# An FFT layer with eight experts behind it: which sorted tile each step of the expert stage works on

## The chip, the cores and the metric

The kernel runs as one program on one core of a Trainium2 chip. The metric is the device time of one execution in microseconds (us), and a kernel's time is the median of its runs. Engines are named as in the profile: PE (TensorE matmul) with PEld (its weight load), DVE (VectorE), ACT (ScalarE), POOL (GpSimd) and SP (SyncE), which here only issues transfers; SPq and POOLq are the sequencers that feed them.

## The reference

Eight sequences of 2496 rows with 256 features go through a Fourier transform along the sequence, a complex 256x256 matrix with bias, a soft threshold and the transform back. Each of the 19968 rows that come out is then sent to one of eight experts, two matrices 256x1024 and 1024x256 with a relu between them, and weighted.

```
X = rfft(x, axis=1)
Yr, Yi = Xr @ w_r - Xi @ w_i + b_r,  Xr @ w_i + Xi @ w_r + b_i
Yr, Yi = soft(Yr, 0.01), soft(Yi, 0.01)
x = irfft(Yr + 1j * Yi).reshape(19968, 256)
e_idx = argmax(x @ w_gate, axis=1)
for e in range(8):
    m = e_idx == e
    out[m] = gate_w[m] * sigmoid(x[m] @ w_output_gate[:, e]) * (relu(x[m] @ w1[e]) @ w2[e])
```

Run on its own inputs, the reference sends 1122, 1344, 1215, 1226, 1333, 1194, 1064 and 1486 rows of the first four sequences to experts 0 to 7, and 2254, 2696, 2453, 2444, 2626, 2443, 2081 and 2971 rows of all eight.

## The kernel before, in words

Values are held as pairs of f16 numbers (a high and a low part), so a product is three matmuls. The Fourier part runs first, sequence by sequence, and writes its rows to `yd` in DRAM. Beside it the expert matrices are scaled, split and written to `wd` in DRAM, 2 MB an expert. The expert stage begins about a third into the program.

**Sorting.** Rows are sorted by expert into tiles of 128. Phase A covers the first four sequences: each expert's rows fill whole pairs of tiles (count // 256 of them), and the first 64 tiles so filled, 32 pairs, are worked on while the last sequences are still being finished. Phase B holds all that is left, each expert's share rounded up to whole tiles, in 99 tiles. So there are 163 tiles (`T_ALL`), worked on in 131 blocks (`BLOCKS`, L41): 32 of two tiles and 99 of one. Which tile number stands for which sorted position is decided by a row of numbers on the chip: tile t takes sorted position t of phase A, or t - 64 of phase B. `plan` (L1062) compares these positions with each expert's start (L1088 to L1092) and so gets `eb`, the expert of each tile; `routing` (L1200) compares the tile number in which a row belongs with the same numbers (`line`, L1224), and the index tables `gidx` and `sidx` for the gathers and scatters come out of that.

**Blocks.** A block gathers the rows of its tiles from `yd` (`gathers`, L1319, an indirect DMA from POOL at L1327), scales and splits them on ACT and DVE (`tokens`, L1333), and turns them with a DMA transpose from SP into `eT` (L1366). `up` (L1447) multiplies with the first matrix (PE, L1458), ACT and DVE make `hh` of it (L1468, L1469), `down` (L1414) multiplies with the second (PE, L1424), ACT scales the result (L1440), and POOL scatters it to the output rows (L1443). In phase B PE's order is two blocks' `up`, then the two `down` of the pair before.

**Weights.** An expert's 2 MB lie in one of three places in SBUF, `wbuf0` to `wbuf2` (`W`); `wplace` (L1291) names the place of block k: blocks 0 to 3 alternate between places 0 and 1, and from block 4 on blocks go round the three. Block k's place was last used by block k - 3 (`before`, L1294). `fetch` (L1298) issues two transfers of 1 MB for each block from SP (L1313), the first half (for `up`) after the earlier block's `up`, the second after its `down`. Each is conditional: a flag in `fl` says whether the block's expert differs from that of the place's earlier block (L1099 to L1104). With the flag at 0 the instruction is issued and moves nothing. SP takes its instructions in program order, and the transposes of L1366 stand between these transfers.

The order of all instructions is worked out ahead by a small simulator in the program (`Issue`), from fixed costs and due times; it doesn't depend on the data.

Of the kernel before, what the change touches and what calls it, by code (L numbers as in the profile page):

```python
# [18 lines left out]
ALU = mybir.AluOpType  # L19
# [5 lines left out]
B, S, D, E, DF = 8, 2496, 256, 8, 1024  # L25
# [3 lines left out]
P3 = 3 * N1  # L29
# [7 lines left out]
T_A = -((-(NA * S - E * 255)) // 256) * 2  # L37
T_B = (N - E) // 128 + E - T_A
T_ALL = T_A + T_B
BLOCKS = [(t, 2) for t in range(0, T_A, 2)] + [(t, 1) for t in range(T_A, T_ALL)]  # L40


def _split(t):
# [4 lines left out]
def tables():  # L48

    n1 = np.arange(N1)  # L50
    k1 = np.arange(K1)
    n2 = np.arange(N2)
    k2 = np.arange(N2)
    a1 = 2 * np.pi * np.outer(n1, k1) / N1
    f1 = np.zeros((3, N1, K1, 3, 2))
    f4 = np.zeros((K1 // 2, 3, 2, 2, 3, N1))
    for s in range(3):
        f1[s, :, :, s, 0] = np.cos(a1)
        f1[s, :, :, s, 1] = -np.sin(a1)
        f4[:, s, :, 0, s, :] = np.cos(a1).T.reshape(K1 // 2, 2, N1)  # L60
        f4[:, s, :, 1, s, :] = -np.sin(a1).T.reshape(K1 // 2, 2, N1)
    f1 = f1.reshape(P3, 120).astype(np.float32)
    f4 = np.concatenate(_split(64 * f4.reshape(120, P3)), axis=1)
    c = np.zeros((128, K1, 128))
    g = np.zeros((128, K1, 128))
    for k in range(K1):
        th = 2 * np.pi * (np.outer(n2, k + 39 * k2) % S) / S
        co, si = np.cos(th), np.sin(th)
        cj = np.where((k2 >= 32) & (k > 0), -1.0, 1.0)
        use = np.where((k == 0) & (k2 > 32), 0.0, 1.0)  # L70
        c[:, k] = np.block([[co * use, -si * use * cj], [si * use, co * use * cj]])
        wr = np.ones(N2)
        wi = np.ones(N2)
        if k == 0:
            wr[33:] = 0.0
            wi[32:] = 0.0
            wi[0] = 0.0
            wr[0] = wr[32] = 0.5
        g[:, k] = np.block([[co.T * wr[:, None], si.T * wr[:, None]], [-si.T * (wi * cj)[:, None], co.T * (wi * cj)[:, None]]])

    mix = np.array([64 * c + 22 * s + q for q in range(NQ) for s in range(3 if q < 20 else 2) for c in range(2)])
    c, g = c[mix], g[:, :, mix]
    ch, cl = _split(64 * c)
    cmat = np.stack([ch, cl], axis=2).reshape(128, K1 * 2 * 128)
    gh, gl = _split(64 * g)
    gmat = np.stack([gh, gl], axis=2).reshape(128, K1 * 2 * 128)

    t = np.zeros((128, NCOL), np.int64)
    real = np.zeros((128, NQ))
    for s in range(3):  # L90
        nq = NQ - 2 * (s > 1)
        rows = slice(s * N1, (s + 1) * N1)
        real[rows, :nq] = 1
        for b in range(B):
            v = 64 * n1[:, None] + np.arange(NQ)[None, :] + 22 * s - S // 2
            t[rows, b * NQ:(b + 1) * NQ] = v + (v >= 0)
    t *= np.tile(real, B).astype(np.int64)
    m16 = np.zeros((128, M16), np.float16)
    m16[:P3, :P3] = np.triu(np.ones((P3, P3)), 1)
    m16[:P3, 128:256] = 1  # L100
    m16[:, 256:432] = t
    m16[:, 432:608] = (real[:, :, None] * (8 - np.arange(8))).reshape(128, 176)
    m16[:, 608:M16 - 384] = np.arange(128 * CB) // CB
    m16[:, M16 - 384:M16 - 256] = np.arange(128)
    m16[:, M16 - 256:M16 - 128] = np.eye(128)

    m16[0:64:32, M16 - 128:M16 - 64] = 2.0 ** 7
    m16[64:128:32, M16 - 64:] = 2.0 ** 7
    return dict(
        f1=np.ascontiguousarray(f1),  # L110
        f4=np.ascontiguousarray(f4),
        cmat=np.ascontiguousarray(cmat),
        gmat=np.ascontiguousarray(gmat),
        m16=m16,
    )
# [36 lines left out]
KW = 4  # L152
# [16 lines left out]
CB = 4  # L169
OL = 2, 3  # L170
KP = 2
NP = K1 // KP
M16 = 608 + 128 * CB + 128 + 256


class Slots:
# [109 lines left out]
def tile_fft_moe(ctx, tc, x, w_r, w_i, b_r, b_i, w_gate, w_og, w1, w2, f1, f4, cmat, gmat, m16, out, dbg=None):  # L286
# [46 lines left out]
    t16 = pc.tile([128, M16], F16, name="t16")  # L333
# [45 lines left out]
    ones = t16[:P3, 128:256]  # L379
    va = t16[:P3, 256:432]  # L380
    eye = t16[:, M16 - 256:M16 - 128]
    iota = t16[:, 608:M16 - 384].rearrange("p (j c) -> p j c", c=CB)
    line = t16[:P3, M16 - 384:M16 - 256].rearrange("p (c j) -> p c j", c=1)
    sel = t16[:, M16 - 128:M16]

    def absmax(m, src):
# [675 lines left out]
    def plan(ph):  # L1062

        if ph == 0:
            fl = shift(cnt[NA - 1], 0, 8, "fl")
            yield
            pf_ = yield from prefix(fl, "pfA")
            lim = small(E + 1, "lim", pool=pc)
            V.tensor_scalar(pf_, pf_, 2.0, None, ALU.mult)
            V.tensor_scalar(lim, pf_, float(T_A), None, ALU.min)  # L1070
            n1 = small(E, "n1", pool=pc)
            V.tensor_tensor(n1, lim[:, 1:], lim[:, :E], ALU.subtract)
            route["n1"] = n1
            off, bound, start = pf_[:, :E], lim[:, 1:], lim
        else:
            ce = shift(cnt[B - 1], 127, 7, "ce")
            V.tensor_tensor(ce, ce, route["n1"], ALU.subtract)
            yield
            start = yield from prefix(ce, "pfB")
            off_ = small(E, "offB", pool=pc)  # L1080
            V.tensor_tensor(off_, start[:, :E], route["n1"], ALU.subtract)
            off, bound = off_, start[:, :E]
        yield
        route[ph] = off, bound
        n = (T_A, T_B)[ph]
        t0 = T_A * ph
        ev = eb[:, t0:t0 + n]
        V.tensor_scalar(ev, iota[:, :n, 0], start[:, 1:2], None, ALU.is_ge)  # L1088
        for e in range(2, E):
            V.scalar_tensor_tensor(ev, iota[:, :n, 0], start[:, e:e + 1], ev, ALU.is_ge, ALU.add)  # L1090
            if e % 2:
                yield  # L1092
        if ph == 0:
            route["fl"] = pc.tile([1, T_ALL], I32, name="flg")
            route["ei"] = pc.tile([1, T_ALL], I32, name="ebi")
            V.memset(route["fl"][:, 0:2 * KW + 1], 1)
        V.tensor_copy(route["ei"][:, t0:t0 + n], ev[0:1])
        fl = lambda a, b, c, d, step: V.tensor_tensor(route["fl"][:, a:b], eb[0:1, a:b], eb[0:1, c:d:step], ALU.not_equal)
        if ph == 0:  # L1099
            fl(4, 2 * KW, 0, 2 * KW - 4, 1)  # L1100
            fl(2 * KW + 1, T_A, 2 * KW - 5, T_A - 6, 1)
        else:
            fl(T_A, T_A + 3, T_A - 6, T_A, 2)
            fl(T_A + 3, T_ALL, T_A, T_ALL - 3, 1)  # L1104
# [95 lines left out]
    def routing(ph, r, gap):  # L1200

        nb = (NA, B)[ph]
        n = (T_A, T_B)[ph]
        yield "ranked", nb - 1
        yield from parts(plan(ph), "D", r, 0.7)
        io.set("plan", ph)
        if ph:
            yield "opened"
            yield "tiles", 0
        for b in range(0, nb, 2):  # L1210
            yield from parts(blocks(ph, b, min(2, nb - b)), "D", r, 0.5)
        io.set("blocks", ph)
        pool = (psm, pools.get("h"))[ph]
        for b in range(nb):
            for q in range(0, NQ, CB):
                m = min(CB, NQ - q)
                yield slots[f"ol{ph}"]
                ol = ring(pool, [P3, 128, CB], F16, f"ol{ph}", OL[ph])
                ob = ring(pool, [P3, CB, n], F16, f"ob{ph}", OL[ph])
                cs = slice(b * NQ + q, b * NQ + q + m)  # L1220
                lc = rlo[:, cs].rearrange("p (o c) -> p o c", o=1).broadcast_to([P3, 128, m])
                bc = blk[:, cs].rearrange("p (c o) -> p c o", o=1).broadcast_to([P3, m, n])
                yield "D", r, 0.147 * m, lambda: V.tensor_tensor(ol[:, :, :m], iota[:P3, :, :m], lc, ALU.is_equal)
                yield "D", r, 0.115 * m, lambda: V.tensor_tensor(ob[:, :m], line[:, :, :n].broadcast_to([P3, m, n]), bc, ALU.is_equal)  # L1224
                io.go(columns(ph, b, q, m, r, ol, ob))
                r += gap * m
                yield max(gap * m - 1.2, 0.0)
        while st.get(("cols", ph), 0) < nb * NQ:
            yield 1.0
        yield slots["gL"]  # L1230
        yield from parts(indices(ph), "D", r, 0.6)
        give("gL")
        io.set("ix", ph)
        for i in range(-(-nb // (512 // n))):
            io.free(route["map", ph, i][0])
        if ph == 0:
            yield "weights"
        yield from parts(factors(ph), "D", r, 0.51)
        io.set("tiles", ph)
# [47 lines left out]

    def place(k, i, shape, dt):
        return pools["w" if i < EARLY[k] else "h"].tile(shape, dt, tag=f"{k}{i}", name=f"{k}{i}")

    def wplace(k):  # L1291
        return k % 2 if k < KW else (k - KW + 2) % 3

    def before(k):  # L1294

# [230 lines left out]
```

## Time and profile before

| | |
|---|---|
| median of three runs | 1447.63 us (1446.49 to 1449.62) |
| the profiled execution: its own time, its span | 1450.28 us, 1448.5 us |
| mean granted TensorE clock | 0.993 |
| busy: PE, PEld, DVE | 1402.4, 1273.4, 978.5 us |
| busy: ACT, POOL | 737.0, 636.1 us |
| `wbuf<-wd` instructions | 262, of 1024 KB each where they move something |
| start of the first and of the last matmul of the expert stage | 552.0 and 1444.0 us |

A row of the timeline gives the start in us, the length in us, the engine, the line, the operation with its output and inputs, the shape and the number of instructions merged; in square brackets stands how long the engine was idle before it and what ended that. A row of the waits gives the engine and line that waited, what released it, the us in total, the times and the longest wait. A row of the windows gives a stretch, its length, the busy time of PE, PEld, DVE, ACT and POOL, the granted clock, the share of the DMA engines' time in use and the GB/s that they moved.

### The profile page before, as it was taken

How to read it: one execution, taken by the hardware profiler on the slowest of the kernel's cores; microseconds unless marked ns; L12 is line 12 of the kernel's file. 1: busy time of each engine (PE TensorE's matmuls, PEld its weight loads, DVE VectorE, ACT ScalarE, POOL GpSimd, SP SyncE). 2: the span in 40 equal slices, each digit the busy share in tenths (PEclk: the TensorE clock that was granted, in tenths of full speed). 3: DMA queues.
4: the chain of work that ended last, by engine and by line, in shares of the span. 5: the costliest groups of instructions: out<-in, count | busy, mean ns of one | idle time of the engine just before them, and what ended most of it. 6: DMA issues, size and time to landing. Idle time of an engine off the chain costs nothing.

```text
span 1448.5 us, 42626 instructions
## 1 busy us (share of the span) xinstructions
PE 1402.4 (97%) x16436; PEld 1273.4 (88%) x16436; DVE 978.5 (68%) x2796; ACT 737.0 (51%) x1413; POOL 636.1 (44%) x729
## 2 busy tenths in 40 slices
PE   4999999999999999999999999999999999999998
PEld 4998887888888888888888888999999999989998
DVE  4888767788998896788888855545545455445452
ACT  4777675778687764433333333333333333333342
POOL 2274565355577563345554333333343333333321
PEclk8999999999999999999999999999999999999999
DMA  7779899998988789977795789674838568386520
GB/s 197 174 174 217 205 224 211 220 223 216 218 211 202 177 238 197 285 193 199 232 231 145 215 207 264 168 218 111 245 94 227 160 167 242 81 244 194 126 58 24
DMA packets 294005, 276.47 MB, mean 191 GB/s; under 512 B 241847, under 2 KB 250169, under 8 KB 282026
## 3 DMA queue, kind: packets, MB, share of 16 engines
q1 hardware_dynamic: 277239, 229.68, 62.5%
q0 software_dynamic: 15872, 42.83, 12.3%
q8 instruction: 129, 2.11, 0.6%
q10 hardware_dynamic: 690, 1.24, 0.3%
q14 instruction: 75, 0.61, 0.1%
HBM read 337.44 MB, written 58.91 MB: 274 GB/s over the span
## 4 chain that ended last, share of the span: by engine, by line
PE 45%; issue 29%; POOL 14%; DVE 6%; DMA 2%; ACT 2%; SPq 1%; POOLq 0%; ACTq 0%; DVEq 0%
PE ps L731 11%; PE ps L1458 9%; PE ps L1424 8%; POOL out L1443 7%; POOL yg L1327 7%; PE ps L623 5%; PE ps L761 3%; PE ps L827 3%; PE ps L701 3%; DMA x<-in_x 1%; PE ps L872 1%; PE ps L666 1%; PE ps L725 1%; PE ps L1253 1%; DVE z L747 1%
## 5 line engine op out<-in xcount | busy, mean ns | idle before, releaser
L1458 PE MATMUL ps<-eT,wbuf 128*128 128x128 f16 (+1 forms) x6288 | 460.9, 233 | 8.4 <-DMA wbuf<-wd 5.6
L1424 PE MATMUL ps<-wbuf,hh 128*128 128x256 f16 x3912 | 453.8, 273 | 0.6 <-DMA wbuf<-wd 0.6
L1458 PEld LDWEIGHTS <-wbuf 128*128 128x128 f16 x6288 | 419.2, 98 | 30.0 <-DMA wbuf<-wd 7.2
L1424 PEld LDWEIGHTS <-hh 128*128 128x128 f16 x3912 | 378.9, 98 | 45.7 <-issue 1.3
L1469 DVE SCALAR_TENSOR_TENSOR hh<-ps,hh 128x512 f16<-128x512 f32 x326 | 224.9, 690 | 275.8 <-ACT hh L1468 275.6
L1468 ACT ACTIVATE hh<-ps 128x512 f16<-128x512 f32 x326 | 194.6, 597 | 294.3 <-PE ps L1458 287.9
L1443 POOL DMA_INDIRECT out<-o,sidx x163 | 163.4, 1003 | 283.4 <-ACT o L1440 259.7
L1327 POOL DMA_INDIRECT yg<-yd,gidx x163 | 161.5, 991 | 252.4 <-DVE yhl L1353 218.2
L731 PE MATMUL ps<-whl,xt 128*128 128x256 f16 x1920 | 223.1, 273 | 0.7 <-ACT xt L716 0.7
L731 PEld LDWEIGHTS <-xt 128*128 128x128 f16 x1920 | 187.6, 98 | 32.2 <-ACT xt L716 1.1
L1440 ACT ACTIVATE o<-ps,facs 128x256 f32<-128x256 f32 x163 | 77.2, 473 | 229.1 <-PE ps L1424 138.4
L1353 DVE SCALAR_TENSOR_TENSOR yhl<-yg,ys,yhl 128x256 f16<-128x256 f32 x163 | 81.8, 508 | 66.2 <-ACT yhl L1352 66.1
L623 PEld LDWEIGHTS ps<-f1t,x 117*128 117x128 f32 (+1 forms) x704 | 86.4, 199 | 18.2 <-issue 15.9
L623 PE MATMUL ps<-f1t,x 117*128 117x120 f32 (+1 forms) x704 | 89.9, 284 | 0.2 <-ACT ste L778 0.2
L1352 ACT ACTIVATE yhl<-yg,ys 128x256 f16<-128x256 f32 x163 | 81.7, 501 | 13.9 <-DVE ys L396 6.2
L751 POOL TENSOR_TENSOR zhl<-z,zhl 128x512 f16<-128x512 f32 x54 | 62.7, 1162 | 52.4 <-ACT zhl L749 50.0
L1028 POOL TENSOR_TENSOR wsp<-wr,wsp 128x512 f16<-128x512 f32 x62 | 74.3, 1198 | 5.2
L761 PE MATMUL ps<-gt,zhl 128*128 128x128 f16 x960 | 65.7, 220 | 7.9 <-DVE zhl L751 3.4
L761 PEld LDWEIGHTS <-zhl 128*128 128x128 f16 x960 | 58.6, 98 | 15.0 <-DVE zhl L751 4.2
L827 PE MATMUL ps<-bdt,f4t 120*117 120x512 f16 x264 | 70.6, 383 | 0.1
L632 ACT ACTIVATE at<-ps,sx 128x480 f16<-128x480 f32 (+1 forms) x88 | 55.7, 650 | 29.1 <-PE ps L623 25.9
L633 DVE SCALAR_TENSOR_TENSOR at<-ps,sx,at 128x480 f16<-128x480 f32 (+1 forms) x88 | 59.3, 696 | 12.5 <-ACT at L632 12.3
(195 smaller groups left out, 1647.8 us busy)
## 6 DMA issues: line engine op xcount, KB each, us to landing
wbuf<-wd SPq DMA_DIRECT2D x262, 1024.0 KB
yd<-yt SPq DMA_DIRECT2D x120, 158.4 KB
x<-in_x SPq DMA_DIRECT2D x114, 156.0 KB
wr<-in_moe_w SPq DMA_DIRECT2D x32, 512.0 KB
wd<-wsp SPq DMA_DIRECT2D x64, 256.0 KB
yg<-yd,gidx POOLq DMA_INDIRECT x163
eT<-yhl SPq DMA_TRANSPOSE x163
out<-o,sidx POOLq DMA_INDIRECT x163
```

The costliest lines, as they stand in the source:

```text
L623: T.matmul(pv[:, dh, :, m * j:m * j + m], xs[:k, j0 + j, 128 * dh:128 * dh + 128], fw, start=True, stop=True)
L731: T.matmul(yp[:, 256 * j:256 * j + 256], xt_[:, v, 2 * dh + j, 64 - 64 * u:192 - 64 * u], whl[:, dh, vw, 256 * u:256 * u + 256], start=Fal ...
L761: T.matmul(bv[:, j], zhl[:, vz, c:c + 128], gt[:, 2 * p + j, v], start=(n == 0), stop=(n == 2))
L827: T.matmul(pt[:P3], w, src[:, :, :, vb_], start=(n == 0), stop=(n == 2))
L1327: yield "G", r + 5.6 * t - 30, 1.0, lambda: G.indirect_dma_start(out=yg, out_offset=None, in_=src, in_offset=bass.IndirectOffsetOnAxis(ap= ...
L1352: yield "A", r - 10, 0.5, lambda: A.activation(yhl[:, 0], yg[:, :256], AF.Copy, scale=s)
L1353: yield "D", r - 10, 0.48, lambda: V.scalar_tensor_tensor(yhl[:, 1], yg[:, :256], s, yhl[:, 0], ALU.mult, ALU.subtract)
L1424: T.matmul(st["pt", t][1][:, :256], hh[:, v, fc, 128 * n:128 * n + 128], w[:, fc // 2, vw, fc % 2], start=(fc == k == 0), stop=(fc == 7 an ...
L1443: yield "G", r - DN, 1.0, lambda: G.indirect_dma_start(out=outs[t % 8], out_offset=bass.IndirectOffsetOnAxis(ap=sidx[:, t:t + 1], axis=0), ...
L1458: T.matmul(pt[:, 128 * m * j:128 * m * (j + 1)], w[:, dh, g // 4, vw, 128 * (g % 4):128 * (g % 4) + 128], eT[:, :m, v, dh], start=(n == 0) ...
L1468: yield "A", r, 0.6, lambda: A.activation(hv[:, 0], pt, AF.Relu)
L1469: yield "D", r, 0.69, lambda: V.scalar_tensor_tensor(hv[:, 1], pt, 0.0, hv[:, 0], ALU.max, ALU.subtract)
```

## The change

The tiles of each phase are handed out otherwise. A new table, `streams()`, gives each tile its sorted position so that the blocks of one place, taken by themselves, run through one third of the sorted tiles: in phase A place 0 gets the first third in order, place 1 the second and place 2 the last; in phase B the same thirds backwards, so that a place enters phase B near the sorted position at which it left phase A. The table is stored in the constant input `m16` where the plain numbers 0 to 127 stood, and both comparisons (for `eb` and in `routing`) read it. `wplace` moves out of the kernel function, unchanged. Flags, fetches, `before` and everything else stay.

```diff
+KA = T_A // 2
...
-    m16[:, 608:M16 - 384] = np.arange(128 * CB) // CB
-    m16[:, M16 - 384:M16 - 256] = np.arange(128)
+    m16[:, 608:LINE] = np.arange(128 * CB) // CB
+    m16[:, LINE:LINE + T_ALL] = streams()
...
-M16 = 608 + 128 * CB + 128 + 256
+LINE = 608 + 128 * CB
+M16 = LINE + T_ALL + T_ALL % 2 + 256
+
+
+def wplace(k):
+    return k % 2 if k < KW else (k - KW + 2) % 3
+
+
+def streams():
+
+    order = np.zeros(T_ALL, np.int64)
+    g = 0
+    for p in range(3):
+        for k in range(KA):
+            if wplace(k) == p:
+                order[2 * k:2 * k + 2] = g, g + 1
+                g += 2
+    g = 0
+    for p in range(3):
+        for k in reversed(range(KA, len(BLOCKS))):
+            if wplace(k) == p:
+                order[BLOCKS[k][0]] = g
+                g += 1
+    return order
...
-    line = t16[:P3, M16 - 384:M16 - 256].rearrange("p (c j) -> p c j", c=1)
+    line = t16[:, LINE:LINE + T_A], t16[:, LINE + T_A:LINE + T_ALL]
...
-        V.tensor_scalar(ev, iota[:, :n, 0], start[:, 1:2], None, ALU.is_ge)
+        V.tensor_scalar(ev, line[ph], start[:, 1:2], None, ALU.is_ge)
...
-            V.scalar_tensor_tensor(ev, iota[:, :n, 0], start[:, e:e + 1], ev, ALU.is_ge, ALU.add)
+            V.scalar_tensor_tensor(ev, line[ph], start[:, e:e + 1], ev, ALU.is_ge, ALU.add)
...
-                yield "D", r, 0.115 * m, lambda: V.tensor_tensor(ob[:, :m], line[:, :, :n].broadcast_to([P3, m, n]), bc, ALU.is_equal)
+                yield "D", r, 0.115 * m, lambda: V.tensor_tensor(ob[:, :m], line[ph][:P3].rearrange("p (c j) -> p c j", c=1).broadcast_to([P3, m, n]), bc, ALU.is_equal)
```

On every engine the instructions stand in the same order as before. One row differs in anything but its line number: SP's load of the constant table, where `t` is the tile `t16` and `in_m` the input `m16`. Before, near the head of SP's program:

```order
6 L359 DMA ct<-in_cmat 128x2560
7 L329 DMA x_278<-in_x 39x1024 x3
8 L363 DMA t_82<-in_m 128x1248
9 L364 DMA wgr<-in_moe_w_gate 128x2x8
10 L365 DMA wgr<-in_moe_w_output_gate 128x2x8
```

and with the change:

```order
6 L383 DMA ct<-in_cmat 128x2560
7 L353 DMA x_278<-in_x 39x1024 x3
8 L387 DMA t_82<-in_m 128x1284
9 L388 DMA wgr<-in_moe_w_gate 128x2x8
10 L389 DMA wgr<-in_moe_w_output_gate 128x2x8
```

The table's load is 36 columns wider, and nothing moved. What changes are numbers: which of the conditional transfers move data, and which rows each gather and scatter takes.

More of the change, by code (lines that the diff above doesn't have):

```diff
@@ L381, in tile_fft_moe @@
     eye = t16[:, M16 - 256:M16 - 128]
-    iota = t16[:, 608:M16 - 384].rearrange("p (j c) -> p j c", c=CB)
-    line = t16[:P3, M16 - 384:M16 - 256].rearrange("p (c j) -> p c j", c=1)
+    iota = t16[:, 608:LINE].rearrange("p (j c) -> p j c", c=CB)
+    line = t16[:, LINE:LINE + T_A], t16[:, LINE + T_A:LINE + T_ALL]
     sel = t16[:, M16 - 128:M16]
@@ L1289, in place @@
         return pools["w" if i < EARLY[k] else "h"].tile(shape, dt, tag=f"{k}{i}", name=f"{k}{i}")
-    def wplace(k):
-        return k % 2 if k < KW else (k - KW + 2) % 3
     def before(k):
```

## The prediction

> **What bounds the kernel now.** First the page: which engine is full, and how much is transferred.
>
> ```profile
> PE 1402.4 (97%) x16436; PEld 1273.4 (88%) x16436; DVE 978.5 (68%) x2796; ACT 737.0 (51%) x1413; POOL 636.1 (44%) x729
> PEclk8999999999999999999999999999999999999999
> DMA packets 294005, 276.47 MB, mean 191 GB/s; under 512 B 241847, under 2 KB 250169, under 8 KB 282026
> q1 hardware_dynamic: 277239, 229.68, 62.5%
> HBM read 337.44 MB, written 58.91 MB: 274 GB/s over the span
> ```
>
> PE is busy 97% of the span at nearly full clock. The change removes transfers and no matmul, so it can gain only what PE loses while it waits for transfers, however many megabytes go. Hence the next view, PE's waits over the whole span, with the longest one for scale and the three that concern the expert stage:
>
> ```profile
> PE ps L422 <- DVE dg L418: 17.6, 4, 10.5
> ...
> PE ps L1458 <- DMA wbuf<-wd: 5.6, 5, 2.2
> ...
> PE ps L1458 <- DMA eT<-yhl: 2.7, 1, 2.7
> ...
> PE ps L1424 <- DMA wbuf<-wd: 0.6, 1, 0.6
> ```
>
> So the ceiling is small: 5.6 + 0.6 us for weights and, if transposes wait behind weights, 2.7 us more. PE's timeline shows where these are and what follows them. First phase A, where a block's `up` begins with the rows of L1458 x24:
>
> ```profile
> 839.98 2.78 PE L1458 MATMUL ps<-eT,wbuf 128*128 128x256 f16 x24
> ...
> 847.84 2.78 PE L1424 MATMUL ps<-wbuf,hh 128*128 128x256 f16 x24
> 853.34 4.16 PE L1458 MATMUL ps<-eT,wbuf 128*128 128x256 f16 x24 [2.72 <-DMA eT<-yhl]
> ...
> 865.49 2.78 PE L1458 MATMUL ps<-eT,wbuf 128*128 128x256 f16 x24
> ...
> 875.97 2.78 PE L1458 MATMUL ps<-eT,wbuf 128*128 128x256 f16 x24
> ```
>
> An undisturbed pair takes 875.97 - 865.49 = 10.48 us. The pair before the wait took 853.34 - 839.98 = 13.36 us, 2.88 too many; the one behind it 12.15 us, 1.67 too many, with no wait in it. Its first 24 matmuls took 4.16 us against 2.78. The windows show why:
>
> ```profile
> 840.00:850.00 10.00, 10.00 (x94) 8.96 (x92) 5.84 (x20) 4.10 (x9) 4.51 (x5) 1.00 1.01 259
> ...
> 855.00:857.00 2.00, 2.00 (x11) 1.45 (x10) 0.69 (x1) 0.58 (x1) 0.00 (x0) 0.50 0.98 398
> ...
> 1292.00:1296.00 4.00, 3.92 (x60) 3.80 (x61) 1.68 (x4) 1.59 (x3) 0.33 (x1) 1.00 0.93 330
> ```
>
> After the 2.72 us wait the granted clock (third number from the end) is 0.50; after the longest weight wait, 2.21 us at 1292, it stays 1.00. So the long wait costs 2.88 + 1.67 = 4.55 us. The Trainium skill, TensorE: Matmul & The Clock Gate, Part 1, puts the fall to half clock behind an idle window of about 3.4 us; by that the 1.67 us would not hang on this wait and would stay, and the gain below would be 1.67 us smaller. Here the clock did fall after 2.7 us, so the row decides and I count it.
>
> Phase B, every place where PE waited for weights, and undisturbed rows for the pace (two blocks' `up` begin at each x96 row):
>
> ```profile
> 925.48 2.85 PE L1458 MATMUL ps<-eT,wbuf 128*128 128x128 f16 x48 [0.70 <-DMA wbuf<-wd]
> 928.92 5.40 PE L1424 MATMUL ps<-wbuf,hh 128*128 128x256 f16 x48 [0.59 <-DMA wbuf<-wd]
> 934.16 5.52 PE L1458 MATMUL ps<-eT,wbuf 128*128 128x128 f16 x96
> ...
> 977.34 5.53 PE L1458 MATMUL ps<-eT,wbuf 128*128 128x128 f16 x96 [0.53 <-DMA wbuf<-wd]
> ...
> 1226.10 2.85 PE L1458 MATMUL ps<-eT,wbuf 128*128 128x128 f16 x48 [1.56 <-DMA wbuf<-wd]
> ...
> 1292.08 2.85 PE L1458 MATMUL ps<-eT,wbuf 128*128 128x128 f16 x48 [2.21 <-DMA wbuf<-wd]
> ...
> 1343.32 5.53 PE L1458 MATMUL ps<-eT,wbuf 128*128 128x128 f16 x96 [0.56 <-DMA wbuf<-wd]
> ...
> 1353.93 5.52 PE L1458 MATMUL ps<-eT,wbuf 128*128 128x128 f16 x96
> ...
> 1428.13 5.52 PE L1458 MATMUL ps<-eT,wbuf 128*128 128x128 f16 x96
> 1433.49 5.40 PE L1424 MATMUL ps<-wbuf,hh 128*128 128x256 f16 x48
> ```
>
> From 1353.93 to 1428.13 nothing waits: 7 pairs of blocks in 74.20 us, 10.60 a pair. From 934.16 to 1428.13 there are 46 pairs, 487.6 us at that pace, and it took 493.97: phase B loses 6.4 us, all around the changes of expert (the four waits sum to 4.9, the rest is restarts and waits under half a microsecond).
>
> **What the change does to the transfers.** From the reference's counts, phase A has 4, 5, 4, 4, 5, 4, 4 and 2 pairs for experts 0 to 7, phase B has 10, 12, 12, 12, 11, 12, 9 and 20 tiles and one empty tile. Before, a change of expert runs through all places: blocks 0, 1, 4 and then 19 more fetch in phase A, 3 for each of 8 experts in phase B: 22 + 24 = 46 blocks, 92 transfers of 1 MB. The page agrees: a transfer is 128 packets of 8 KB, 92 x 128 = 11,776, and it has 294005 - 282026 = 11,979 packets of 8 KB or more, some 200 of them instructions. After, places 0, 1 and 2 hold 11, 11 and 10 pairs, so experts 0-1-2, 2-3-4 and 5-6-7: 9 fetches. In phase B, backwards, 33 tiles each, place 0 runs 2-1-0 (2 is there already), place 1 5-4-3-2 (4 was there), place 2 7-6-5 (7 is there): 2 + 4 + 2 = 8. So 17 blocks fetch and 29 stop fetching, at 2.1 MB each 60.8 MB less. The new ones are blocks 0, 1, 4, 6, 11, 16, 18, 26 and 28, then 33, 60, 65, 93, 97, 101, 124 and 129: no two neighbours after the first two, and in phase B at least four blocks, 21 us, apart.
>
> **Is a lone fetch hidden?** A place is used by every third block, so between its last use and the next one PE has two whole blocks, 10.6 us in phase B and 21 us in phase A, and each half has this room for itself. The first fetch of a group before is such a lone one. For block 101, whose `up` began inside 1276.43's row:
>
> ```profile
> 1266.76 2.31 SPq L1313 DMA_DIRECT2D wbuf<-wd  x2
> ...
> 1269.50:1274.00 4.50, 4.50 (x60) 4.21 (x58) 3.70 (x13) 1.59 (x3) 0.99 (x1) 1.00 0.86 263
> ...
> 1276.43 5.52 PE L1458 MATMUL ps<-eT,wbuf 128*128 128x128 f16 x96
> ```
>
> The second of these instructions, near 1269.0, is its first half; at 263 GB/s 1.05 MB take 4.0 us, so it was there by 1274, five microseconds before need, and no first block of a group shows a wait of a microsecond. Only second and third blocks do, since 6.3 MB at about 295 GB/s take 21 us. After the change there are none of those.
>
> **The sum, against the profiled execution's 1450.28 us** (span 1448.5):
>
> 1. Phase B: -6.4 us. Bounds: the waits alone, 4.9, and the whole 6.4.
> 2. Entry into B, 925 to 929: the 0.59 us wait of L1424 is for block 34's second half, which is not fetched any more: -0.6. The 0.70 us wait stays for the most part:
>
> ```profile
> 923.47 6.38 SPq L1313 DMA_DIRECT2D wbuf<-wd  x6
> ```
>
> SP reaches block 35's conditional transfer (the second of the six) only after block 34's second half, which waits for its place to be given up, and reading the flags takes SP its time also when nothing is moved. I take -0.3 for the shorter issue and bound it by 0 and -0.7. Together -0.9.
> 3. The wait at 853: -4.55 us, if it goes. The transposes of that block came late in SP's order, behind two weight halves:
>
> ```profile
> 838.86 2.20 SPq L1313 DMA_DIRECT2D wbuf<-wd  x2
> 841.16 6.12 SPq L1366 DMA_TRANSPOSE eT<-yhl  x3
> ```
>
> The two halves are block 27's second and block 28's first. At 259 GB/s they occupy the DMA for 8.1 us. Block 27 no longer fetches, block 28 does; so 4.05 us of the transfer ahead go, and the wait was 2.72. It should vanish, with 1.3 us to spare, and with it the fall of the clock. Bounds: 0 and -4.55.
> 4. The last tile: before, the last scatter is that of the empty tile and writes no row; after, the empty tile is the first of place 2 in phase B, and the last scatter writes 128 rows, 131 KB. At 263 GB/s that is 0.5 us; bounds 0 and 1. +0.5.
> 5. DVE's comparisons read other columns of the same table in the same number; the table's load grows by 72 B a row, 9 KB. DVE has 98 us of room in the stretch where they lie:
>
> ```profile
> 552.00:919.00 367.00, 363.26 (x3442) 322.97 (x3441) 268.59 (x823) 146.66 (x277) 157.43 (x169) 1.00 0.83 217
> ```
>
> So 0, with PE's 363.26 of 367 us as cover; without it a slower `line` comparison would cost its own length.
>
> Sum: -6.4 - 0.9 - 4.55 + 0.5 = -11.35, so 1438.9 us for an execution like the profiled one. That one stands 2.65 us over the median of the runs and above all three. If the difference is the profile's own, the median after is 1447.63 - 11.35 = 1436.3; if the profiled execution merely waited more than the others, those have less to lose and all end at 1438.9. I can't tell these apart and take the middle, **1437.5 us**, 0.7% faster.
>
> **The rivals.**
>
> *The wait at 853 stays.* Block 28's half still goes out just before the transposes of 841.16, whose pace SP's 6.12 us for three shows to be that of a full queue. If their delay comes from any transfer ahead of them, not from two, term 3 falls away: 1437.5 + 4.55 = 1442.0. The Trainium skill, DMA: Bandwidth & Descriptors, Queues, rings and completion order, says that each DMA engine consumes a queue's descriptors in ring order; by that rule the transposes still stand behind what is left, as this rival has it. Against it: the arithmetic above leaves 1.3 us. Chance 0.12.
>
> *The unprofiled runs never had that wait.* It is one event and its price hangs on the clock; the runs spread over 3.1 us. Then the median loses 6.4 + 0.9 - 0.5 = 6.8: 1440.8. Chance 0.09.
>
> *The change doesn't do what it says, or new small waits eat it*: the flags compare each block with block k - 3, as `wplace` has it, and the count of 46 agrees with the trace, so I see no way for the first. For the second, eight lone fetches in phase B would have to cost over a microsecond each. About 1447. Chance 0.03.
>
> *Slower: lone fetches don't fit.* The tiles of a place change expert at moments at which nothing else pauses, so a half that needs longer than its 10.6 us stops PE at once. It decides from 10.6 us a half, 99 GB/s; being measurably slower takes the gain of 11.35 and 3 us more, so 1.8 us for each of the eight fetches, halves of 12.4 us, or 85 GB/s. Time: 1450.5. The rows show 259 to 398 GB/s whenever weights move. Chance 0.03.
>
> **Chances and range.** The forecast has 0.73. With 0.2%, about 2.9 us, as what a measurement of this kernel can tell from no change, forecast and the first two rivals are faster: 0.94; same 0.03; slower 0.03. The range goes from 1436.3, less the 1.1 us by which the lowest run lies under the median and the 0.9 us by which terms 2 and 4 can come out better, about 1434, to the first rival with half a microsecond on it, 1442.5.
>
> **What would show it.** HBM reads fall by 61 MB to about 277, queue q1 to 169 MB. PE's waits for `wbuf` shrink from 6.2 us to about 0.4, at the entry into B; pairs keep 10.48 and 10.60 us. No wait for `eT` near 850 and no granted clock under 1.00 there. The last scatter ends half a microsecond later after its start. A wait for `wbuf` at blocks 60, 65, 93, 97, 101, 124 or 129 would make the account of the lone fetch wrong; a wait for `eT` at 850, term 3; a pace other than 10.60 without waits would mean that PE's rate depends on something that I left out.

## The result and the profile after

On the chip of the first profile the changed kernel takes 1436.87 us (median of four runs, 1436.6 to 1438.22) against 1448.62 us (four runs, 1446.49 to 1451.93): a ratio of 0.9919, 95% interval 0.9898 to 0.9940. 1437.5 us had been forecast. The profiled execution after took 1436.6 us, span 1434.8.

The page after, the lines that answer to those of before:

```profile
PE 1399.4 (98%) x16436; PEld 1273.4 (89%) x16436; DVE 978.2 (68%) x2796; ACT 738.6 (51%) x1413; POOL 636.3 (44%) x729
DMA packets 285652, 215.66 MB, mean 150 GB/s; under 512 B 240918, under 2 KB 249240, under 8 KB 281097
q1 hardware_dynamic: 268887, 168.87, 49.6%
HBM read 337.45 MB, written 58.91 MB: 276 GB/s over the span
```

The transfers fell by 60.81 MB, as forecast, and the packets of 8 KB or more from 11,979 to 4,555, which is 58 transfers of 128 packets fewer. The last line did not move; more of that below. PE's waits, the longest and the only one left that concerns the expert stage:

```profile
PE ps L446 <- DVE dg L442: 10.9, 3, 10.0
...
PE ps L1479 <- DMA wbuf<-wd: 0.4, 1, 0.4
```

And PE's timeline at the places of the prediction (L1479 is `up`, L1445 `down`):

```profile
837.97 2.78 PE L1479 MATMUL ps<-eT,wbuf 128*128 128x256 f16 x24
...
848.45 2.78 PE L1479 MATMUL ps<-eT,wbuf 128*128 128x256 f16 x24
...
858.92 2.78 PE L1479 MATMUL ps<-eT,wbuf 128*128 128x256 f16 x24
...
918.60 2.85 PE L1479 MATMUL ps<-eT,wbuf 128*128 128x128 f16 x48 [0.38 <-DMA wbuf<-wd]
921.29 5.40 PE L1445 MATMUL ps<-wbuf,hh 128*128 128x256 f16 x48
926.53 5.52 PE L1479 MATMUL ps<-eT,wbuf 128*128 128x128 f16 x96
...
1424.73 2.84 PE L1479 MATMUL ps<-eT,wbuf 128*128 128x128 f16 x48
```

Laid beside the rows of before, stretch by stretch, they give the whole difference of the two spans. The rows are the starts of `up` of blocks 26, 28, 36 and 130; before, the last of these and the one `down` behind it are:

```profile
1438.73 2.85 PE L1458 MATMUL ps<-eT,wbuf 128*128 128x128 f16 x48
1441.41 2.84 PE L1424 MATMUL ps<-wbuf,hh 128*128 128x256 f16 x24
```

A single `down` (24 matmuls) follows the last `up`. So in phase B PE runs two blocks' `up` and then the two `down` of the same pair, not of the pair before, as the description of the kernel has it.

| stretch | before | after | difference | forecast |
|---|---|---|---|---|
| to block 26 | 839.98 | 837.97 | -2.0 | 0 |
| block 26 to 28 (the wait at 853) | 25.51 | 20.95 | -4.56 | -4.55 |
| block 28 to 36 (entry into phase B) | 68.67 | 67.61 | -1.06 | -0.9 |
| block 36 to 130 (phase B) | 504.57 | 498.20 | -6.37 | -6.4 |
| block 130 to the end | 9.77 | 10.07 | +0.30 | +0.5 |

Phase B now runs at 498.20 / 47 = 10.60 us a pair from end to end, the pace of the undisturbed rows. The clock at the old place of the wait, third number from the end:

```profile
851.00:853.00 2.00, 2.00 (x21) 1.80 (x19) 0.97 (x2) 1.02 (x2) 0.84 (x1) 1.00 0.97 397
```

The last scatter starts 3.8 us before the end of the span, against 3.5 before:

```profile
1431.04 0.97 POOL L1464 DMA_INDIRECT out<-o,sidx  x1 [4.34 <-ACT o L1461]
```

The 2.0 us ahead of block 26 arise before the expert stage: its first matmul stands at 552.0 before and 550.0 after, and from there to block 26 both take 288.0 us. On a fourth chip four kernels that are alike up to that point began it at 546.3, 546.9, 548.0 and 549.2, so it varies by execution by more than these 2.0 us, and the table doesn't count them as the change's.

### The profile page after: what moved, and what is told of

The parts are those of the page before. It is cut to its first block, busy times and chain, and to the rows that moved or that the text cites. A ratio compares the mean times of both kernels' runs of the same rounds, so it can differ in the third digit from the quotient of the medians.

```text
span 1434.8 us, 42626 instructions
## 1 busy us (share of the span) xinstructions
PE 1399.4 (98%) x16436; PEld 1273.4 (89%) x16436; DVE 978.2 (68%) x2796; ACT 738.6 (51%) x1413; POOL 636.3 (44%) x729
## 3 DMA queue, kind: packets, MB, share of 16 engines
q1 hardware_dynamic: 268887, 168.87, 49.6%
q0 software_dynamic: 15872, 42.83, 12.1%
q10 hardware_dynamic: 690, 1.24, 0.3%
HBM read 337.45 MB, written 58.91 MB: 276 GB/s over the span
## 4 chain that ended last, share of the span: by engine, by line
PE 46%; issue 29%; POOL 14%; DVE 6%; DMA 2%; ACT 1%; POOLq 0%; SPq 0%; ACTq 0%; DVEq 0%
PE ps L755 11%; PE ps L1479 9%; PE ps L1445 8%; POOL out L1464 7%; POOL yg L1348 7%; PE ps L647 5%; PE ps L851 3%; PE ps L785 3%; PE ps L725 3%; DMA x<-in_x 1%; PE ps L896 1%; PE ps L690 1%; PE ps L749 1%; PE ps L1277 1%; DVE z L771 1%
## 5 line engine op out<-in xcount | busy, mean ns | idle before, releaser
L1479 PE MATMUL ps<-eT,wbuf 128*128 128x128 f16 (+1 forms) x6288 | 458.9, 232 | 0.4 <-DMA wbuf<-wd 0.4
L1445 PE MATMUL ps<-wbuf,hh 128*128 128x256 f16 x3912 | 453.2, 273 | 0.0
L1479 PEld LDWEIGHTS <-wbuf 128*128 128x128 f16 x6288 | 418.9, 98 | 19.9 <-DMA wbuf<-wd 0.6
L1445 PEld LDWEIGHTS <-hh 128*128 128x128 f16 x3912 | 378.8, 98 | 44.2 <-issue 0.2
L770 ACT ACTIVATE zhl<-ps,sc 128x512 f32<-128x512 f32 x80 | 54.8, 685 | 25.6 <-PE ps L755 22.1
```

The lines of the kernel that those rows point to most:

```text
L1445: T.matmul(st["pt", t][1][:, :256], hh[:, v, fc, 128 * n:128 * n + 128], w[:, fc // 2, vw, fc % 2], start=(fc == k == 0), stop=(fc == 7 an ...
L1479: T.matmul(pt[:, 128 * m * j:128 * m * (j + 1)], w[:, dh, g // 4, vw, 128 * (g % 4):128 * (g % 4) + 128], eT[:, :m, v, dh], start=(n == 0) ...
```

## The experiments

The theory to test: PE lost time where three neighbouring blocks fetched at once, and a lone fetch is hidden. The rivals: PE's loss follows the megabytes moved (volume); or the time is saved by the new order of the tiles itself, through the rows that gathers and scatters touch (order). Most kernels are the changed one with a few more writes of 1 into the fetch flags; a block then fetches the expert that already lies in its place. The twelve runs were made on three further chips, four on each, and each, but for the second profile of the kernel before, has its ratio to the kernel before on the same chip.

**The old fetches under the new order.**

```diff
             fl(2 * KW + 1, T_A, 2 * KW - 5, T_A - 6, 1)
+            V.memset(route["fl"][:, 18:23:2], 1)
+            V.memset(route["fl"][:, 52:57:2], 1)
...
             fl(T_A + 3, T_ALL, T_A, T_ALL - 3, 1)
+            V.memset(route["fl"][:, 74:77], 1)
+            V.memset(route["fl"][:, 133:136], 1)
...
```

> The changed kernel with its new order of tiles, but the fetch flags are also set to 1 at every block at which the kernel before fetched (contents of the places stay the same; it only fetches an expert again that already lies there). Fetches: the 46 blocks of before and 7 of the change's own, four of them in a row at blocks 65 to 68. Theory (groups of three neighbouring fetches are what PE waits for): the waits come back in their old places, phase B from block 36 to block 130 about 504 to 506 us instead of 498.2, the wait near 850 with its clock fall back (blocks 25 to 28 in 36.0 us instead of 31.4), about 1447 us in all. Rival (the new order of tiles itself saves the time, by the rows that gathers and scatters touch): 1437 us, phase B 498.2.

Ratio 1.0043 (1.0022 to 1.0065): with the fetches back the kernel is as slow as before and a little slower. PE's waits:

```profile
PE ps L1494 <- DMA wbuf<-wd: 9.4, 4, 4.6
...
PE ps L1494 <- DMA eT<-yhl: 1.0, 2, 0.7
```

Three of the waits stand in old places (blocks 44, 91, 103; the one of block 112 is missing), and the longest at the four fetches in a row of blocks 65 to 68:

```profile
1100.08 5.30 PE L1494 MATMUL ps<-eT,wbuf 128*128 128x128 f16 x48 [4.55 <-DMA wbuf<-wd]
...
1302.02 4.19 PE L1494 MATMUL ps<-eT,wbuf 128*128 128x128 f16 x48 [2.98 <-DMA wbuf<-wd]
```

The order alone therefore saves nothing that these runs can tell; that rival is out. Two of the expectations fail. Phase B took 521.0 us, not 504 to 506: the four in a row, slower clocks behind the two longest waits and the stops told of below come on top. And the wait near 850 came back as 0.29 us with no fall of the clock, blocks 25 to 28 in 31.9 us and not in 36.0.

**As many fetches, but apart.**

```diff
+            V.memset(route["fl"][:, 40:49:4], 1)
...
+            V.memset(route["fl"][:, 69:86:4], 1)
+            V.memset(route["fl"][:, 88:89], 1)
+            V.memset(route["fl"][:, 101:122:4], 1)
+            V.memset(route["fl"][:, 137:150:4], 1)
```

> The changed kernel with 22 fetches more, none beside another: 15 blocks fetch in phase A (22 before, 9 in the change) and 24 in phase B (24 before, 8 in the change), all at least two blocks apart, nearly all three or four. Theory (bunching): a lone fetch is hidden, so phase B stays at 498.2 us and the whole at 1437, within 1 us. Rival (volume: PE's loss follows the megabytes): phase B back near 504.6, about 1444 to 1447 in all.

**No fetches after the first of each place.**

```diff
+            V.memset(route["fl"][:, 10:T_A], 0)
...
+            V.memset(route["fl"][:, T_A:T_ALL], 0)
```

> The changed kernel that leaves out every fetch after the first in each place (most tiles are multiplied by another expert's weights; the work of every engine stays the same). Theory: the remaining lone fetches already cost nothing, so 1437 us within 1 us and phase B 498.2. Rival (each lone fetch costs a few tenths in contention): some 2 to 4 us faster. The wait of 0.4 us at the entry into phase B stays in both, since it hangs on SP's order and not on data.

The two ran on one chip, with ratios of 0.9936 (0.9910 to 0.9961) and 0.9928 (0.9902 to 0.9953). The page and the waits of the first, 24 blocks of phase B fetching:

```profile
DMA packets 291988, 261.80 MB, mean 181 GB/s; under 512 B 241622, under 2 KB 249944, under 8 KB 281801
```

```profile
PE ps L1487 <- DMA wbuf<-wd: 0.4, 1, 0.4
```

and the waits of the second, with 186.30 MB in all:

```profile
PE ps L1481 <- DMA wbuf<-wd: 0.4, 1, 0.4
```

So 75 MB more, and PE waits for weights in neither, but for the 0.4 us at the entry. Volume is out as the cause of these waits. The times were not as expected, though: phase B took 511.9 and 506.5 us, not 498.2, and none of that is a wait for weights. In the profile of the kernel before on this chip it took 511.6 us, so by its time phase B gained nothing here from the fetches' standing apart, and these two runs can't tell by time whether a lone fetch costs a few tenths. That is settled by the run with groups of two below, on a chip without such stops: 22 blocks of phase B fetch there, 245.02 MB in all, and it takes the 498.20 us of the changed kernel with its 8. On this chip PE's weight loads stop in phase B and the profile shows no release (`issue`). In the run with fetches apart, and in the one without:

```profile
PEld L1487 <- issue: 12.1, 32, 0.6
```

```profile
PEld L1481 <- issue: 6.2, 22, 0.6
```

The stops of phase B begin 2.1 to 2.5 us into a pair's `up`, none comes after the pair of blocks 118 and 119, and they don't follow the number of fetches: there they sum to 12.1 us with 24 fetches apart and 5.7 us with none, but to 5.9 us in the kernel before on the same chip, also with 24, and to 6.3 us in the run with the old fetches, with 30. What they are stays open. Because of them the runs of the second and third chip are judged by waits and stretches, not by the whole.

**The kernel before again.**

> The kernel before once more, for a second profile. If the wait for the transposes near 850 and its clock fall are a property of the kernel, blocks 25 to 28 take 36.0 us again (change: 31.4); if they are an event of one execution (the second rival), 31.4 to 33. The start of the expert stage, 552.0 in the one profile of before and 550.0 in the changed kernel's, should differ again by 2 us if the change moved it, and lie anywhere within some 2 us if it varies by execution.

```profile
PE ps L1458 <- DMA wbuf<-wd: 4.7, 3, 2.4
...
PE ps L1458 <- DMA eT<-yhl: 1.8, 2, 1.1
```

```profile
852.20 2.78 PE L1458 MATMUL ps<-eT,wbuf 128*128 128x256 f16 x24 [1.08 <-DMA eT<-yhl]
```

The wait for the transposes is there, but 1.08 us long instead of 2.72, and no slower clock follows: those 24 matmuls take 2.78 us. Blocks 25 to 28 take 32.7 us, 1.2 more than undisturbed, not 4.55. The expert stage starts at 551.1; three changed kernels on this chip start it at 548.4, 549.1 and 550.8. Together with the spread of the fourth chip that fits chance, but one profile a kernel can't rule out a small shift.

**One fetch more, at block 27.**

```diff
+            V.memset(route["fl"][:, 54:55], 1)
```

> The changed kernel with one fetch more: block 27, between the change's own at 26 and 28, so the transposes issued near 839 stand behind two weight halves again and not one. Theory: the wait for eT near 849 returns, 2 to 3 us, and behind it the granted clock falls and costs 1.7 us more: blocks 25 to 28 in 35 to 36.5 us instead of 31.4, about 1441 in all. Rival (that wait came from gathers and scatters that happened to crowd): no wait, 31.4 us, 1437.

SP and PE around it:

```profile
836.39 2.20 SPq L1335 DMA_DIRECT2D wbuf<-wd  x2
838.70 5.33 SPq L1388 DMA_TRANSPOSE eT<-yhl  x3
```

```profile
837.51 2.78 PE L1480 MATMUL ps<-eT,wbuf 128*128 128x256 f16 x24
...
847.99 2.24 PE L1480 MATMUL ps<-eT,wbuf 128*128 128x256 f16 x19
```

The two halves are back ahead of the transposes, and PE doesn't wait: 10.48 us from one `up` to the next. The expectation fails. Ratio 0.9952 (0.9933 to 0.9971).

**The change in phase A alone, and in phase B alone.**

```diff
-    g = 0
-    for p in range(3):
-        for k in reversed(range(KA, len(BLOCKS))):
...
+    order[T_A:] = np.arange(T_B)
```

> The change in phase A alone; phase B keeps the plain order of before. Theory: phase A gains its 4.55 us (blocks 25 to 28 in 31.4 us), the entry into B fetches at blocks 32, 33 and 34 as before (blocks 28 to 36 in 68.7 us), phase B keeps its 504.6, the last scatter stays the empty one: about 1443. Rival (the parts are not independent, phase B's waits are set by what phase A leaves queued): another sum by over 2 us.

```diff
-    g = 0
-    for p in range(3):
-        for k in range(KA):
...
+    order[:T_A] = np.arange(T_A)
```

> The change in phase B alone; phase A keeps the plain order. Theory: phase A keeps its wait near 853 and the clock fall (blocks 25 to 28 in 36.0 us), phase B 498.2 us, at the entry two fetches at blocks 32 and 33, so block 34 waits no more (blocks 28 to 36 in 67.6 to 68.2): about 1441.5. Rival as for the change in phase A alone: another sum by over 2 us.

Phase A alone: ratio 1.0000 (0.9985 to 1.0015), with no wait in phase A and these left, from the entry (the one for `eT` and that of L1440) and from phase B:

```profile
PE ps L1474 <- DMA wbuf<-wd: 2.5, 2, 1.7
...
PE ps L1474 <- DMA eT<-yhl: 0.8, 1, 0.8
...
PE ps L1440 <- DMA wbuf<-wd: 0.6, 1, 0.6
```

Phase B alone: ratio 0.9964 (0.9950 to 0.9977), and the mirror image:

```profile
PE ps L1474 <- DMA eT<-yhl: 0.5, 1, 0.5
...
PE ps L1474 <- DMA wbuf<-wd: 0.4, 1, 0.4
```

Each half of the change takes away the waits of its phase. In time, phase B carries the gain on that chip, 5.3 us of 1461.0, and phase A shows none, where 4.55 us had been expected: the wait that it removes was 0.5 us in the one profile that has it there, with no fall of the clock. Whether the two add up can't be read from these, since the whole change wasn't run on that chip and phase B held some 13 us of stops without a release.

**Groups of three, of two, and all.** Seven groups of neighbouring fetches in phase B of the changed kernel: three from an odd block, three from an even one, two from an odd one; then every block. The first group of each as it is written (the others begin 8, 28, 36, 44, 64 and 72 blocks later), and the last kernel's line:

```diff
+            V.memset(route["fl"][:, 73:76], 1)
...
+            V.memset(route["fl"][:, 74:77], 1)
...
+            V.memset(route["fl"][:, 73:75], 1)
...
+            V.memset(route["fl"][:, T_A:T_ALL], 1)
```

> The changed kernel with seven groups of three neighbouring fetches set in phase B, each group beginning at an odd block (41, 49, 69, 77, 85, 105, 113), contents unchanged. In the kernel before, two groups began at odd blocks (89, 101) and cost 1.7 and 2.4 us; five began at even ones and cost 0 to 0.9. Theory (an even block's up has 15.7 us between its place's release and its start, an odd one's 10.5, and the third fetch of an odd group is odd): 1.7 to 2.4 us for each group, phase B 510 to 515 instead of 498.2, about 1449 to 1454. Rival (the two costs were chance of queueing): as many waits as the even groups have, about 502.

> The changed kernel with seven groups of three neighbouring fetches in phase B, each beginning at an even block (42, 50, 70, 78, 86, 106, 114), one block later than in the run whose groups begin at odd ones, which waited 16.2 us for wbuf. Theory (the third block decides, and an even third block has 15.7 us between release and use, an odd one 10.5): 0 to 0.9 us a group as in the kernel before, PE waits for wbuf 2 to 5 us in all. Rival (the parity doesn't matter): about 16 us again.

> The changed kernel with seven groups of two neighbouring fetches at odd blocks and the next (41 and 42, 49 and 50, 69 and 70, 77 and 78, 85 and 86, 105 and 106, 113 and 114). Theory (it takes three, since only the third block's halves queue behind more than 4 MB): PE waits for wbuf 0.4 to 1 us in all. Rival (any neighbouring fetch costs): 3 to 8 us.

> The changed kernel with every block of phase B fetching its 2.1 MB, contents unchanged: where a lone fetch's room ends. Theory (transfers then set the pace): at 295 to 395 GB/s a block takes 5.3 to 7.1 us instead of 5.3, so the 94 blocks from 36 to 130 take 560 to 668 us instead of 498, most likely near 600, and the whole is 60 to 160 us slower. Rival (the queue hides them as it hides lone ones): within 10 us.

PE's waits for weights, in the same order (ratios 1.0120, 1.0060 to 1.0180; 0.9959, 0.9941 to 0.9977; 0.9919, 0.9902 to 0.9935; 1.1164, 1.1139 to 1.1189):

```profile
PE ps L1486 <- DMA wbuf<-wd: 16.2, 8, 3.6
```

```profile
PE ps L1486 <- DMA wbuf<-wd: 4.5, 5, 1.8
```

```profile
PE ps L1486 <- DMA wbuf<-wd: 0.4, 1, 0.4
```

```profile
PE ps L1480 <- DMA wbuf<-wd: 128.8, 37, 7.5
```

Two neighbouring fetches, the first at an odd block, cost nothing: phase B took 498.20 us again. Pairs that begin at an even block were not run. Three cost 4.5 us of waiting in seven groups from an even block and 16.2 from an odd one (0.4 of each is the entry's). In time phase B took 504.4 us with the even groups, 6.2 more than without and close to what the kernel before lost, and 536.5 us with the odd ones, where 510 to 515 had been expected: four falls of the clock and 12 us of stops without a release come on top of the waits there.

The expectation for the even groups came out in its sum, but not in its mechanism, that the third block decides. With odd groups all seven waits for first halves stand at the third block (43, 51, 71, 79, 87, 107, 115). With even groups three of the four stand at the second (51, 79, 115) and one at the third (88). The longest of these, at block 51 of the group 50 to 52:

```profile
1003.59 2.85 PE L1486 MATMUL ps<-eT,wbuf 128*128 128x128 f16 x48 [1.83 <-DMA wbuf<-wd]
```

What the runs have in common is the odd block with other fetches ahead of it: an odd block's `up` follows its place's release by 10.5 us, an even one's by 15.7 us. With every block fetching, 36 of the 37 waits of `up` stand at odd blocks. The odd run was on the third chip and the others on the fourth, so part of the factor between 4.5 and 16.2 may be the chip. The parity itself is not: within the kernel before, on the first chip, the odd groups (89 and 101) cost 1.7 and 2.4 us and the even ones at most 0.9, and in the run with the change in phase A alone, on the third chip, phase B's only waits for weights are those of the same two odd groups.

With every block fetching, phase B goes at the transfers' pace: 668.3 us for 94 blocks, 7.1 us for 2.10 MB, 295 GB/s of weights, the slow end of what was expected.

**The changed kernel again**, on the fourth chip.

> The changed kernel once more, since the chips of the experiments give the kernel before 8 to 12 us more than the first one did. There PE stops for 0.1 to 0.7 us in most pairs of blocks of phase B, with no release that the profile shows (listed as issue), in every kernel, the one without fetches too. Theory (these stops are the chip's and not the weights'): the change still gains 6 to 10 us against before on the same chip, PE waits for wbuf only 0.4 us and for eT not at all, blocks 25 to 28 take 31.4 us, and phase B exceeds 498.2 us only by such stops. Rival (the stops belong to the change): they are much fewer in the kernel before, and the gain is under 3 us.

Ratio 0.9931 (0.9914 to 0.9947), medians 1435.28 and 1447.12 us. Phase B 498.20 us, blocks 25 to 28 31.44 us, and of waits only

```profile
PE ps L1479 <- DMA wbuf<-wd: 0.4, 1, 0.4
```

This chip shows none of the stops without a release, and the gain is that of the first chip.

## Why the prediction was right, and where not

*What bounds the kernel.* Right. 61 MB went, and in the expert stage PE gained its waits and what had followed from them. Phase B now runs at the undisturbed pace from end to end, so fewer fetches can't shorten it further.

*Phase B, -6.4 us.* Right to the tenth (-6.37), and its cause is shown: the waits come back with the old fetches, stay away when about as many stand apart or in twos from odd blocks, and return with groups of three. "Second and third blocks" was right too; what it left out is that nearly all the waits stand at odd blocks, whose `up` follows sooner on their place's release. Its reason was mis-sized: 295 GB/s is all that the DMA engines moved in that stretch. The six halves of blocks 101 to 103 alone went, by their packets, from 1269 to 1295, about 26 us and 240 GB/s, not 21 us.

*A lone fetch is hidden.* Shown by 24 lone fetches in phase B without a wait, by all of them left out without a gain in waits, and in time by the changed kernel, whose 8 lone fetches leave phase B at the undisturbed pace. The rival that they don't fit would begin at 99 GB/s; with every block fetching the weights still make 295.

*The entry, -0.9.* -1.06. The first wait stayed at 0.38 us, as SP's order has it, and stays also where nothing is fetched; the second went.

*The wait at 853, -4.55.* The profiled executions agree (-4.56), and yet this is the term that doesn't stand. In the five profiles with two weight halves ahead of those transposes, blocks 25 to 28 lost 4.55 us (before), 1.24 (before again), 0.61 (change in B alone), 0.45 (the old fetches) and nothing (block 27). With one half ahead, or none, it was nothing in all nine. So the wait was seen only with the second half ahead, and that half doesn't suffice. The step that fails is the arithmetic from 8.1 us of transfers to a wait of 2.72: in all five profiles the DMA engines moved the same 308 to 315 GB/s in the 8 us from block 26's `up` on. The profiles part behind that. In the next 2.5 us, with the transposes, gathers and scatters left, the engines moved 72 and 75 GB/s in the two profiles of before, 116 and 114 in the next two and 133 in the run with block 27. The first and the last of these:

```profile
847.98:850.48 2.50, 2.50 (x25) 2.22 (x23) 1.58 (x9) 1.58 (x3) 0.38 (x1) 1.00 0.65 72
```

```profile
845.51:848.01 2.50, 2.50 (x26) 2.24 (x24) 1.58 (x9) 1.58 (x3) 0.38 (x1) 1.00 1.21 133
```

What slows this stretch, the gathers and scatters or the chip, was not separated.

So the median's agreement with the forecast is in part luck. The terms that stand sum to 7.1 us (-6.37, -1.06, +0.30). That the first chip's runs gained 11.75 us all the same, and the fourth's 11.84, means that their runs of before lost some 4 to 5 us to this wait or to something else; only one execution was profiled on the first, and none of before on the fourth. The second rival had the right idea for the other chips: an event with a price that varies.

*The last scatter, +0.5.* +0.30: within its bounds.

*HBM reads.* Wrong: the page's line stayed where it was, at 337.45 MB, where I had expected 277. Queue q1 fell to 168.87 MB, as expected.

## What to carry to other kernels

Before a saving of transfers is priced, look at when the transfers stand: here a fetch alone, or in twos from an odd block, cost nothing, groups of three up to 3.6 us of waiting, and fetching at every block 1.8 us a block. When a few buffers change their contents at the same moment because the work is sorted, give each buffer its own run through the sorted work. And a wait that a profile shows once is a sample: take a second profile before its length enters a sum.

## What the runs showed of the hardware that was not expected

**The clock falls after some short waits and not after others as long, and each fall costs about the same.** In the run with groups of three from odd blocks:

```profile
968.73 2.85 PE L1486 MATMUL ps<-eT,wbuf 128*128 128x128 f16 x48 [2.16 <-DMA wbuf<-wd]
...
1130.15 4.48 PE L1486 MATMUL ps<-eT,wbuf 128*128 128x128 f16 x48 [2.49 <-DMA wbuf<-wd]
...
1175.54 0.44 PE L1486 MATMUL ps<-eT,wbuf 128*128 128x128 f16 x5 [0.32 <-issue]
1177.46 4.40 PE L1486 MATMUL ps<-eT,wbuf 128*128 128x128 f16 x48 [1.47 <-DMA wbuf<-wd]
...
1336.74 2.85 PE L1486 MATMUL ps<-eT,wbuf 128*128 128x128 f16 x48 [2.29 <-DMA wbuf<-wd]
...
1382.53 4.48 PE L1486 MATMUL ps<-eT,wbuf 128*128 128x128 f16 x48 [2.34 <-DMA wbuf<-wd]
```

```profile
1130.20:1132.20 2.00, 2.00 (x24) 2.00 (x25) 0.54 (x1) 0.00 (x0) 0.00 (x0) 0.62 0.92 381
...
1177.50:1179.50 2.00, 2.00 (x28) 2.00 (x29) 1.25 (x6) 0.10 (x1) 0.00 (x0) 0.74 1.02 380
...
968.80:970.80 2.00, 2.00 (x37) 2.00 (x38) 0.56 (x1) 0.46 (x1) 0.00 (x0) 1.00 0.94 380
```

Waits of 2.49 and 1.47 us (the latter with a stop of 0.32 us two microseconds ahead of it) were followed by a granted clock of 0.62 and 0.74 in these stretches, and the 48 matmuls after the wait of 2.34 us took 4.48 us as well. After waits of 2.16 and 2.29 us they took the usual 2.85 us, and so they did after the 2.38 us of the second profile of before. Length alone doesn't decide, then. Where the clock fell after a wait under 3 us, PE lost 1.6 to 1.7 us more, in before, in this run, in the one with the old fetches and in the one with the change in phase A alone. The Trainium skill, TensorE: Matmul & The Clock Gate, Part 1, gives an idle window of about 3.4 us for the fall and says that the window runs freely, so that the number of slow matmuls at a kernel's start varies by run. These rows vary too; the fall came after waits well under 3.4 us.

**The page's HBM line doesn't follow conditional transfers.** It reads 337.44 or 337.45 MB in every run, with 186 MB moved and with 407; so it seems to count them whether or not they move. The line of the DMA packets is the one that follows the flags.
